# Top-k attention with expert routing on one core: the steps of the search one place further apart

## The chip, the core and the metric

The kernel runs on one core of a Trainium2 chip. The core has five engines that each take their own instructions in order and wait for one another only through semaphores: TensorE (PE in the profile, with its weight loads as PEld), VectorE (DVE), ScalarE (ACT), GpSimd (POOL) and SyncE (SP, which here only starts transfers). The metric is the device time of one execution in microseconds (us), lower is better.

## The reference

Two blocks follow one another, all in float32. The first is attention over 8 batches, 8 heads, 576 rows and head size 64, in which each row keeps only its 32 largest scores:

```python
scores = scale * np.matmul(q, k.transpose(0, 1, 3, 2))
kth = np.partition(scores, -top_k, axis=-1)[..., -top_k:-top_k + 1]
scores = np.where(scores >= kth, scores, -1000000000.0)
attn = softmax(scores)             # over the last axis
x = np.matmul(attn, v)             # heads side by side: 4608 x 512
```

The second block routes each of the 4608 rows of x to the best of 8 experts, keeps the 80 rows with the largest gate weight of each expert, and sends those through two matrix products (512 to 1024 to 512); all other rows of the output are zero.

## The kernel before

**Work and staging.** Two heads of one batch form a head pair; there are 32, numbered n. The 576 rows of a head pair are cut into four tiles of 128 rows and one of 64. A *unit* i is one head of one 128-row tile; the 64-row tile holds both heads side by side in one unit. So a head pair has 9 units (four times two, and one), and the whole attention has NU = 288. Only after it come routing and experts (from about 868 us on), which the change does not touch.

**What is done for a tile.** `front` (L226) multiplies q and k into the PSUM tile `sp`, and ScalarE copies the scores to `s` (L233). `parts` takes the 8 largest of each sixth of a row into `cand` (L241). `search` finds from `cand` the 24 largest (L252, L260). Then ScalarE makes `sign` (L257), which marks the scores above the 24th, and counts them; GpSimd multiplies `y = s * sign` (L263); VectorE takes the 8 largest of `y` into `w` (L265), and `pick` (L268) chooses the 32nd largest score among these as threshold. `below` makes the `mask`: on GpSimd (L279) for units with an even number, on ScalarE (L277) for odd ones. `turn_w` transposes the scores and adds the masks on TensorE (L315, L320) into `ab` (PSUM, one buffer) and `cc` (PSUM, two buffers), and ScalarE takes the exponential into `wT` (L322 from `cc`, L324 from `ab`). `back` multiplies with v (L335), into free columns of the same `cc`. `over` takes the reciprocal of the row sums on VectorE (L347, tile `z_all`), and `divide` copies `cc` times that into `xn` on ScalarE (L358). Only then is this buffer of `cc` free. `norm` stores `xn`, transposes it (L201, L375) and multiplies it with the gate weights (L380, L387). `turn` transposes q and k of the next head pair (L201) and ScalarE copies them out as `both` (L214). All of `sp`, the transposes of `turn` and of `norm` and the small product share one PSUM buffer.

**The order** is written out by hand. The program is recorded in *steps*; step i works on unit i in `parts` and `search`, on earlier units in the later stages, and on a later one in `front` (unit i + 4). Each letter of a string stands for one piece of work, and `back` says how many units behind i it is:

```python
back = dict(a=0, b=1, c=1, d=1, e=1, y=2, g=3, h=4, m=4, H=3, M=3)
for c in "GybGcGdGeGGzag" if i % 2 else "GGbghHmMyGcGdGeGza":
```

G is a piece of L241; a, b, c, d, e are the steps of `search` up to the sign, which ScalarE gets with e; y is the product on GpSimd, g is L265, h and H are the two picks, m and M the two masks, z the reciprocal. After the letters a step issues `turn_w` of the tile whose last unit is i - 4, `divide` of the tile whose reciprocal was just taken, `front` and `back` (of the tile of unit i - 5). Every engine executes its share of this one order without overtaking. For each head pair I call the five tiles' weight turns W0 to W4; W4 is that of the 64-row tile. `cc` has two buffers, so W2 takes the buffer of W0, W3 that of W1, and so on through the head pairs.

SBUF tiles come from pools: `s` has 5 buffers (one for the two heads of a tile), `sign` 2, `mask` 3, and the small tiles 4.

Of the kernel before, what the change touches and what calls it, by code (L numbers as in the profile page):

```python
# [9 lines left out]
F32 = mybir.dt.float32  # L10
# [17 lines left out]
def kernel(  # L28
# [21 lines left out]
    P = 128  # L50
# [98 lines left out]
    class Attention:  # L149


        def __init__(self, stack, lean):
            self.lean = lean
            pool = lambda name, bufs, **kw: stack.enter_context(tc.tile_pool(name=name, bufs=bufs, **kw))
            self.nat, self.qkp, self.rows = pool("nat", 1), pool("qkp", 2), pool("rows", 2)
            self.small, vpool = pool("small", 4), pool("vpool", 1)
            self.ps_s, self.ps_w, self.ps_c = (pool(n, k, space=PSUM) for n, k in (("ps_s", 1), ("ps_w", 1), ("ps_c", 2)))
            self.qk, self.turned, self.lg = {}, {}, {}
            self.s, self.top, self.cnt, self.y, self.mask, self.w, self.xn = ({} for _ in range(7))
            self.thr, self.z = thr_all, z_all  # L160
            self.odd = set()


            self.vb = []
            for j in range(1 if lean else 3):
                t = vpool.tile([P, NK, 2, D + 1], F32, name=f"vb{j}")
                nc.gpsimd.memset(t[:, :, :, D : D + 1], 1.0)
                nc.gpsimd.memset(t[: P - TL, NF, :, :], 0.0)
                self.vb.append(t)

            self.xT = vpool.tile([P, NK * P], F32, name="xT")
            nc.gpsimd.memset(self.xT[:, S:], 0.0)

        def load(self, n, b, hp):
            one = bass.ds(b, 1)
            tiles = []
            for name, src in (("qn", q), ("kn", k)):
                t = self.nat.tile([P, NK, 2, D], F32, name=name, tag=name)
                for h in range(2):
                    nc.sync.dma_start(  # L180
                        t[:, 0:NF, h, :],
                        src[one, 2 * hp + h, : NF * P, :].rearrange("o (c p) d -> p (o c) d", p=P))
                nc.sync.dma_start(
                    t[0:TL, NF, :, :], src[one, 2 * hp : 2 * hp + 2, NF * P :, :].rearrange("o h p d -> p (o h) d"))
                tiles.append(t)
            t = self.vb[n % len(self.vb)]
            for h in range(2):
                nc.sync.dma_start(
                    t[:, :NF, h, :D], v[one, 2 * hp + h, : NF * P, :].rearrange("o (c p) d -> p (o c) d", p=P))
            nc.sync.dma_start(  # L190
                t[P - TL :, NF, :, :D], v[one, 2 * hp : 2 * hp + 2, NF * P :, :].rearrange("o h p d -> p (o h) d"))
            self.qk[n] = tiles

        def four(self):
            return self.ps_s.tile([P, 4, 512], F32, name="sp", tag="sp")
# [20 lines left out]
        def front(self, n, t):  # L216

            qT, kT = self.turned[n]
            m = P if t < NF else TL
            i = n * UPP + 2 * t  # L220
            ps = self.four()
            for j in range(2):
                for h in range(2):
                    d = slice(D * h, D * h + D)
                    o = ps[:, 2 * h + j, :HS] if t < NF else ps[TL * h : TL * h + TL, j, :HS]
                    nc.tensor.matmul(o, lhsT=qT[d, t * P : t * P + m], rhs=kT[d, j * HS : (j + 1) * HS], start=True, stop=True)  # L226
            g = 2 if t < NF else 1
            s = self.rows.tile([P, 2 * S], F32, name="s", tag="s", bufs=2 if self.lean else 5)
            for h in range(g):
                self.s[i + h] = s[:, h * S : (h + 1) * S]  # L230
            for j in range(0, 2 * g, 2 if i == 0 else 2 * g):
                w = 2 if i == 0 else 2 * g
                nc.scalar.activation(s[:, j * HS : (j + w) * HS].rearrange("p (j c) -> p j c", c=HS), ps[:, j : j + w, :HS],  # L233
                                     Act.Copy, scale=TINY)
# [10 lines left out]
        def search(self, i):  # L245

            s, cand = self.s[i], self.top[i]
            top = self.top[i] = self.small.tile([P, G0 // 8 - 1, 8], F32, name="top", tag="top")
            w9 = self.small.tile([P, 16], F32, name="w9", tag="w9")
            for r in range(G0 // 8):  # L250
                dst = top[:, r, :] if r < G0 // 8 - 1 else w9[:, :8]
                nc.vector.max(out=dst, in_=cand)  # L252
                if r == G0 // 8 - 1:

                    sign = self.rows.tile([P, S], BF16, name="sign", tag="sign")
                    cnt = self.small.tile([P, 1], F32, name="cnt", tag="cnt")
                    nc.scalar.activation(sign, s, Act.Sign, bias=w9[:, 7:8], scale=-1.0, accum_out=cnt)  # L257
                yield
                if r < G0 // 8 - 1:
                    nc.vector.match_replace(out=cand, in_to_replace=dst, in_values=cand, imm_value=LOW)  # L260
                    yield
            y = self.rows.tile([P, S], F32, name="y", tag="y")
            nc.gpsimd.tensor_tensor(out=y, in0=s, in1=sign, op=Alu.mult)  # L263
            yield
            nc.vector.max(out=w9[:, 8:], in_=y)  # L265
            yield
            pick = self.small.tile([P, TOP_K - G0 + 1], F32, name="pick", tag="pick")
            nc.vector.scalar_tensor_tensor(out=pick, in0=past, scalar=cnt, in1=w9[:, 7:], accum_out=self.thr[:, i : i + 1],  # L268
                                           op0=Alu.is_equal, op1=Alu.mult)
            yield  # L270

        def below(self, i):

            self.top.pop(i)
            self.mask[i] = self.rows.tile([P, S], BF16, name="mask", tag="mask", bufs=3)
            if i in self.odd:
                nc.scalar.activation(self.mask[i], self.s[i], Act.Relu, bias=self.thr[:, i : i + 1], scale=-1.0)  # L277
                return
            nc.gpsimd.tensor_scalar(self.mask[i], self.s[i], self.thr[:, i : i + 1], None, op0=Alu.is_lt)  # L279
# [147 lines left out]
        def run(self, slow):  # L427

            units = []
            for n in range(NP):  # L430
                for t in range(NF):
                    units += [(n, t, 0), (n, t, 1)]
                units.append((n, NF, 2))
            self.odd = set(range(1, NU, 2))
            first, second = {}, {}
            later = []
            due = []
            drawn = []
            ready = {}

            def whole(i):
# [3 lines left out]
            def step(i, last):  # L445
                if 0 <= i < NU:
                    n, t, h = units[i]
                    if t == 2 and h == 1 and n + 2 < NP:
                        self.load(n + 2, *divmod(n + 2, HP))
                    if t in (1, 3) and h == 0 and slow and n:  # L450
                        slow.pop(0)()
                    if t == 0 and h == 0 and n + 1 < NP:
                        due.append(n + 1)
                    first[i] = self.parts(i)


                back = dict(a=0, b=1, c=1, d=1, e=1, y=2, g=3, h=4, m=4, H=3, M=3)
                for c in "GybGcGdGeGGzag" if i % 2 else "GGbghHmMyGcGdGeGza":
                    if c == "G":
                        if 0 <= i < NU:  # L460
                            next(first[i])
# [3 lines left out]
                            second[i] = self.search(i)  # L465
                            next(second[i])
                    elif c == "z":
                        for u in drawn:
                            self.over(*u)
                    elif c in "mM":  # L470
                        if 0 <= i - back[c] < NU:
                            self.below(i - back[c])
                    elif i - back[c] in second:
                        next(second[i - back[c]])
                done = list(drawn)
                drawn.clear()

                def back():
                    if whole(i - 5):
                        self.back(*units[i - 5][:2])  # L480
                        drawn.append(units[i - 5][:2])


                rest = whole(i - 4) and units[i - 4][2] == 2
                if rest:
                    back()
                if whole(i - 4):
                    self.turn_w(*units[i - 4][:2])
                for u in done:
                    self.divide(*u)  # L490

                ends = [(n, range(NK) if n < NP - 1 else range(NF) if t < NF else range(NF, NK))
                        for n, t in done if t == NF or (n == NP - 1 and t == NF - 1)]
# [20 lines left out]
                    ready[later[-1]] = 0  # L514

            with tc.manual_schedule():
                self.load(0, 0, 0)
                self.load(1, *divmod(1, HP))
                nc.sync.dma_start(wg, moe_w_gate.rearrange("(c p) e -> p c e", p=P))
                self.turn(0)  # L520
                i = -4
                while i < NU + 6 or later:
                    step(i, i >= NU + 5)
                    i += 1
            assert not slow and not due

        def batch(self, b):

            for hp in range(HP):
                self.load(hp, b, hp)  # L530
                self.turn(hp)
                for t in range(NK):
                    self.front(hp, t)
# [381 lines left out]
```

## Time and profile before

| | us |
|---|---|
| median of 3 runs (lowest, highest) | 994.47 (993.04, 995.51) |
| the profiled execution | 994.13 |
| its span, first to last instruction | 992.4 |
| busy in the span: PE, DVE, ACT, POOL | 881.3, 804.6, 798.2, 627.3 |
| first and last GpSimd mask start | 22.12, 855.23 |
| mean granted TensorE clock | 0.983 of full speed |

The profile is of one execution. Its own time lies 1.7 us above its span (launch and end), and 0.3 us below the median of the runs. Busy times of different engines overlap. The row of a group of instructions gives their count, the busy time and the mean duration of one, and then the idle time of that engine just before them with what ended it; a row of the waits gives the waiting instruction, what released it, the time in total, how often, and the longest. In the timeline, an instruction begins often some 0.1 us before the one ahead of it on the same engine has ended, so that the distance of two starts is shorter than the duration.

### The profile page before, as it was taken

How to read it: one execution, taken by the hardware profiler on the slowest of the kernel's cores; microseconds unless marked ns; L12 is line 12 of the kernel's file. 1: busy time of each engine (PE TensorE's matmuls, PEld its weight loads, DVE VectorE, ACT ScalarE, POOL GpSimd, SP SyncE). 2: the span in 40 equal slices, each digit the busy share in tenths (PEclk: the TensorE clock that was granted, in tenths of full speed). 3: DMA queues.
4: the chain of work that ended last, by engine and by line, in shares of the span. 5: the costliest groups of instructions: out<-in, count | busy, mean ns of one | idle time of the engine just before them, and what ended most of it. 6: DMA issues, size and time to landing. Idle time of an engine off the chain costs nothing.

```text
span 992.4 us, 35679 instructions
## 1 busy us (share of the span) xinstructions
PE 881.3 (89%) x13368; PEld 710.3 (72%) x13368; DVE 804.6 (81%) x4928; ACT 798.2 (80%) x1652; POOL 627.3 (63%) x474
## 2 busy tenths in 40 slices
PE   5899999999989999999899999999899998689996
PEld 3677777777767777777677777777677776578896
DVE  5798989898989898999989898989898989471110
ACT  3899999999989999999899999999899999501110
POOL 3677767676767777777677676766677777402111
PEclk9999999999999999999999999999999999979999
DMA  3445453333323233333111122222222200084921
GB/s 72 102 123 133 126 135 91 92 92 92 93 76 77 75 87 86 88 90 92 46 41 44 44 50 50 51 50 49 49 50 50 50 13 14 16 339 147 368 85 29
DMA packets 167797, 85.76 MB, mean 86 GB/s; under 512 B 117696, under 2 KB 154560, under 8 KB 167616
## 3 DMA queue, kind: packets, MB, share of 16 engines
q1 hardware_dynamic: 166592, 80.78, 29.1%
q0 software_dynamic: 1024, 2.62, 0.9%
q8 instruction: 107, 1.75, 0.7%
q14 instruction: 74, 0.61, 0.2%
HBM read 63.19 MB, written 20.19 MB: 84 GB/s over the span
## 4 chain that ended last, share of the span: by engine, by line
DVE 46%; PE 26%; ACT 15%; POOL 7%; issue 5%; DMA 1%; POOLq 0%; SPq 0%; DVEq 0%; ACTq 0%
DVE cand L241 15%; DVE w L265 11%; DVE cand L260 6%; PE cc L335 5%; DVE top L252 5%; ACT sign L257 5%; POOL y L263 5%; PE sp L226 4%; PE yp L799 4%; DVE pick L268 3%; ACT wT L324 3%; ACT mask L277 3%; PE sp L201 2%; DVE w L252 2%; POOL mask L279 2%
## 5 line engine op out<-in xcount | busy, mean ns | idle before, releaser
L241 DVE MAX8 cand<-s 128x8 f32<-128x96 f32 x1728 | 400.6, 246 | 9.0 <-ACT s L233 8.8
L263 POOL TENSOR_TENSOR y<-s,sign 128x576 f32<-128x576 f32 x288 | 365.3, 1280 | 65.9 <-ACT sign L257 65.9
L279 POOL TENSOR_SCALAR mask<-s,thr_all 128x576 bf16<-128x576 f32 x144 | 247.9, 1722 | 178.3 <-DVE pick L268 175.4
L335 PEld LDWEIGHTS cc<-vb,wT 128*64 128x64 f32 x5760 | 182.8, 139 | 113.6 <-ACT wT L324 100.1
L265 DVE MAX8 w<-y 128x8 f32<-128x576 f32 x288 | 216.4, 752 | 45.8 <-POOL y L263 45.8
L335 PE MATMUL cc<-vb,wT 128*64 128x65 f32 x5760 | 205.2, 226 | 42.7 <-ACT wT L324 42.7
L257 ACT ACTIVATE sign<-s,w 128x576 bf16<-128x576 f32 x288 | 225.2, 782 | 7.1 <-POOL y L263 3.0
L226 PE MATMUL sp<-both 64*128 64x288 f32 (+1 forms) x1280 | 203.2, 437 | 17.5 <-ACT part L387 9.5
L233 ACT ACTIVATE s<-sp 128x1152 f32<-128x1152 f32 (+1 forms) x161 | 167.4, 1040 | 12.2 <-PE sp L226 9.9
L315 PE MATMUL ab<-ident,s 128*128 128x128 f32 x1148 | 176.2, 283 | 0.0
L324 ACT ACTIVATE wT<-ab 128x1024 f32<-128x1024 f32 (+1 forms) x159 | 149.1, 937 | 0.0
L226 PEld LDWEIGHTS sp<-both 64*128 64x128 f32 (+1 forms) x1280 | 106.1, 180 | 56.4 <-ACT part L387 11.4
L315 PEld LDWEIGHTS ab<-ident,s 128*128 128x128 f32 x1148 | 127.9, 142 | 11.6 <-issue 0.9
L252 DVE MAX8 top<-cand 128x8 f32<-128x48 f32 x576 | 116.0, 201 | 4.5
L277 ACT ACTIVATE mask<-s,thr_all 128x576 bf16<-128x576 f32 x144 | 112.4, 781 | 6.9 <-DVE pick L268 6.5
L320 PEld LDWEIGHTS <-mask 128*128 128x128 bf16 x1440 | 94.2, 98 | 31.9 <-POOL mask L279 29.2
L260 DVE MATCH_REPLACE8 cand<-top,cand 128x48 f32<-128x48 f32 x576 | 110.9, 193 | 0.0
L358 ACT ACTIVATE xn<-cc,z_all 128x64 f32<-128x64 f32 (+1 forms) x320 | 86.6, 320 | 1.2 <-DVE z_all L347 0.8
L315 PE MATMUL cc<-ident,s 128*128 128x128 f32 x288 | 79.1, 275 | 0.0
L322 ACT ACTIVATE wT<-cc 128x256 f32<-128x256 f32 (+1 forms) x160 | 56.9, 356 | 16.8 <-PE cc L320 15.5
L268 DVE SCALAR_TENSOR_TENSOR pick<-past,cnt,w 128x9 f32<-128x9 f32 x288 | 60.3, 223 | 0.3 <-ACT xn L358 0.3
L257 ACT ACTIVATION_READ_ACCUMULATOR sign<-s,w 128x1 f32 x288 | 58.7, 204 | 0.0
(187 smaller groups left out, 909.4 us busy)
## 6 DMA issues: line engine op xcount, KB each, us to landing
w<-in_moe_w_dram SPq DMA_DIRECT2D x10, 2048.0 KB, 11.6
w<-in_moe_w_dram SPq DMA_DIRECT2D x24, 512.0 KB, 4.6
out_dram<-zero SPq DMA_DIRECT2D x9, 1024.0 KB, 6.5
qn<-in_q_dram SPq DMA_DIRECT2D x64, 128.0 KB, 2.5
kn<-in_k_dram SPq DMA_DIRECT2D x64, 128.0 KB, 2.5
vb<-in_v_dram SPq DMA_DIRECT2D x64, 128.0 KB, 2.7
xd<-xn SPq DMA_DIRECT2D x32, 256.0 KB, 3.8
qn<-in_q_dram SPq DMA_DIRECT2D x32, 32.0 KB, 2.3
```

The costliest lines, as they stand in the source:

```text
L226: nc.tensor.matmul(o, lhsT=qT[d, t * P : t * P + m], rhs=kT[d, j * HS : (j + 1) * HS], start=True, stop=True)
L233: nc.scalar.activation(s[:, j * HS : (j + w) * HS].rearrange("p (j c) -> p j c", c=HS), ps[:, j : j + w, :HS], Act.Copy, scale=TINY)
L241: nc.vector.max(out=cand[:, j, :], in_=s[:, j * S // NG : (j + 1) * S // NG])
L252: nc.vector.max(out=dst, in_=cand)
L257: nc.scalar.activation(sign, s, Act.Sign, bias=w9[:, 7:8], scale=-1.0, accum_out=cnt)
L260: nc.vector.match_replace(out=cand, in_to_replace=dst, in_values=cand, imm_value=LOW)
L263: nc.gpsimd.tensor_tensor(out=y, in0=s, in1=sign, op=Alu.mult)
L265: nc.vector.max(out=w9[:, 8:], in_=y)
L279: nc.gpsimd.tensor_scalar(self.mask[i], self.s[i], self.thr[:, i : i + 1], None, op0=Alu.is_lt)
L315: nc.tensor.matmul(dst[h][c], lhsT=sc[:, keys[c]], rhs=ident, start=c == 0 or (c == NF and h == 0), stop=False, is_transpose=True, skip_gr ...
L324: nc.scalar.activation(wT[:, : g * NF, :], ab.rearrange("p h c r -> p (h c) r")[:, : g * NF, :], Act.Exp, scale=scale / TINY)
L335: nc.tensor.matmul(cc[r : r + TL, o], lhsT=wT[:, h * NF + c if c < NF else 2 * NF + h, r : r + TL], rhs=vb[:, c, h if t < NF else r // TL, ...
```

## The change

It moves stages of the order to later steps, adds buffers, and splits the loading of v from that of q and k. No instruction is added or removed in the attention; their order on each engine changes. The product y moves from 2 to 3 units behind, L265 from 3 to 4; the pick and mask of odd units from 3 to 5, those of even units stay at 4 (the letters h, m and H, M change places in parity). `turn_w` moves from 4 to 6 units behind, `back` from 5 to 7, and the reciprocal comes two steps after `back` in place of one, earlier within its step; `divide` is issued ahead of `turn_w` of the same step, where it was behind it. The loading of v for head pair n + 2 is issued two steps later.

```diff
-            self.small, vpool = pool("small", 4), pool("vpool", 1)
+            self.small, vpool = pool("small", 7), pool("vpool", 1)
...
-            s = self.rows.tile([P, 2 * S], F32, name="s", tag="s", bufs=2 if self.lean else 5)
+            s = self.rows.tile([P, 2 * S], F32, name="s", tag="s", bufs=2 if self.lean else 7)
...
-                    sign = self.rows.tile([P, S], BF16, name="sign", tag="sign")
+                    sign = self.rows.tile([P, S], BF16, name="sign", tag="sign", bufs=3)
...
-            self.mask[i] = self.rows.tile([P, S], BF16, name="mask", tag="mask", bufs=3)
+            self.mask[i] = self.rows.tile([P, S], BF16, name="mask", tag="mask", bufs=4)
...
+            LT = 6
...
-            drawn = []
+            drawn = [[], [], []]
...
                     if t == 2 and h == 1 and n + 2 < NP:
                         self.load(n + 2, *divmod(n + 2, HP))
+                    if t == 3 and h == 1 and n + 2 < NP:
+                        self.load_v(n + 2, *divmod(n + 2, HP))
...
-                back = dict(a=0, b=1, c=1, d=1, e=1, y=2, g=3, h=4, m=4, H=3, M=3)
-                for c in "GybGcGdGeGGzag" if i % 2 else "GGbghHmMyGcGdGeGza":
+                back = dict(a=0, b=1, c=1, d=1, e=1, y=3, g=4, h=5, m=5, H=4, M=4)
+                for c in "GybGczGdGeGGag" if i % 2 else "GGbghHmMyGcGdzGeGa":
...
                     elif c == "z":
-                        for u in drawn:
+                        for u in drawn[0]:
                             self.over(*u)
...
-                done = list(drawn)
-                drawn.clear()
+                done = drawn.pop(0)
+                drawn.append([])
+                for u in done:
+                    self.divide(*u)
 
                 def back():
-                    if whole(i - 5):
-                        self.back(*units[i - 5][:2])
-                        drawn.append(units[i - 5][:2])
+                    if whole(i - LT - 1):
+                        self.back(*units[i - LT - 1][:2])
+                        drawn[1].append(units[i - LT - 1][:2])
 
-                rest = whole(i - 4) and units[i - 4][2] == 2
+                rest = whole(i - LT) and units[i - LT][2] == 2
                 if rest:
                     back()
-                if whole(i - 4):
-                    self.turn_w(*units[i - 4][:2])
-                for u in done:
-                    self.divide(*u)
+                if whole(i - LT):
+                    self.turn_w(*units[i - LT][:2])
...
-                while i < NU + 6 or later:
-                    step(i, i >= NU + 5)
+                while i < NU + LT + 3 or later:
+                    step(i, i >= NU + LT + 2)
```

The function `load_v` holds the three transfers of v that stood at the end of `load`, and is called right behind `load` for the first two head pairs.

More of the change, by code (lines that the diff above doesn't have):

```diff
@@ L185, in load, with load_v @@
                 tiles.append(t)
+            self.qk[n] = tiles
+        def load_v(self, n, b, hp):
+            one = bass.ds(b, 1)
             t = self.vb[n % len(self.vb)]
@@ L191, in load @@
                 t[P - TL :, NF, :, :D], v[one, 2 * hp : 2 * hp + 2, NF * P :, :].rearrange("o h p d -> p (o h) d"))
-            self.qk[n] = tiles
         def four(self):
@@ L516, in run @@
             with tc.manual_schedule():
-                self.load(0, 0, 0)
-                self.load(1, *divmod(1, HP))
+                for n in range(2):
+                    self.load(n, *divmod(n, HP))
+                    self.load_v(n, *divmod(n, HP))
                 nc.sync.dma_start(wg, moe_w_gate.rearrange("(c p) e -> p c e", p=P))
@@ L530, in batch @@
                 self.load(hp, b, hp)
+                self.load_v(hp, b, hp)
                 self.turn(hp)
```

## The prediction

> **What bounds the kernel now.** I read the page first, then the waits of the steady stretch, then the timelines of GpSimd, TensorE and ScalarE.
>
> ```profile
> PE 881.3 (89%) x13368; PEld 710.3 (72%) x13368; DVE 804.6 (81%) x4928; ACT 798.2 (80%) x1652; POOL 627.3 (63%) x474
> ```
>
> No engine is full over the span, and four are close together. The waits between 60 and 845 us say how they hold one another (us, times, longest):
>
> ```profile
> POOL mask L279 <- DVE pick L268: 166.7, 134, 3.3
> ...
> POOL y L263 <- ACT sign L257: 45.9, 58, 2.1
> DVE w L265 <- POOL y L263: 37.8, 43, 2.1
> ...
> ACT both L214 <- PE sp L201: 21.1, 29, 2.3
> DVE z_all L347 <- PE cc L335: 19.4, 15, 1.3
> ```
>
> GpSimd, the least busy engine, waits most, and its timeline shows a ring:
>
> ```profile
> 322.15 1.72 POOL L279 TENSOR_SCALAR mask<-s,thr_all 128x576 bf16<-128x576 f32 x1 [1.14 <-DVE pick L268]
> 323.83 2.52 POOL L263 TENSOR_TENSOR y<-s,sign 128x576 f32<-128x576 f32 x2
> 327.45 1.72 POOL L279 TENSOR_SCALAR mask<-s,thr_all 128x576 bf16<-128x576 f32 x1 [1.10 <-DVE pick L268]
> ```
>
> Mask, two products, then 1.10 us for L265 and the pick that frees the next mask: 5.31 us for two units. The masks go from 22.12 to 855.23 us in 143 rounds, 5.83 us each. The 0.52 between are rounds in which the second product waits for its sign (0.6 to 2.1 us), because ScalarE is late with it: behind `both`, the transposes of `norm`, or TensorE.
>
> [...]
>
> **What the change takes away.** The sign gets a whole step more before its product, so the 45.9 us and the 37.8 us behind them (the same delay, counted once: about 46) should go; the reciprocal comes later behind `back`, so most of the 19.4 us should go too. The mask's own wait stays: mask, product, product, L265, pick is still one ring. In the new order both picks stand ahead of GpSimd's mask, where one did: 0.19 us more (starts of the two picks at 327.06 and 327.25). That ring is then 5.50 us. VectorE and GpSimd alone would give 143 x (5.83 - 5.50) = 47 us less.
>
> **What it adds: a wait for `cc`.** A weight turn may write `cc` only after `divide` of the tile two turns earlier. Before, this was done a step and more ahead; the timeline's groups on `cc` have, among those that waited for it, one line:
>
> ```profile
>   ACT xn L358: 0.8, 1
> ```
>
> One wait of 0.8 us in 785 us. In the new order the lead is one step: `turn_w` of a tile comes 6 steps after its last unit, its `divide` 9, and the turn that needs its buffer 10 (before: 4, 6 and 8). For W0, which follows the one-unit W4, it is the same step: `divide` of W3 stands directly ahead of W0's exponential on ScalarE. W4 has the same with `divide` of W2. So ScalarE and TensorE form a ring: s (L233), then masks and signs, `xn`, then TensorE's turn from its first `cc` matmul, `front`, then the next s. The pieces, from the rows:
>
> ```profile
> 605.99 0.27 PE L315 MATMUL cc<-ident,s 128*128 128x128 f32 x1
> ...
> 606.92 0.22 PE L320 MATMUL cc<-huge,mask 128*128 128x128 bf16 x1
> ...
> 607.30 1.24 PE L226 MATMUL sp<-both 64*128 64x288 f32 x8
> 608.53 1.39 PE L335 MATMUL cc<-vb,wT 128*64 128x65 f32 x40
> ```
> ```profile
> 607.18 0.38 ACT L322 ACTIVATE wT<-cc 128x256 f32<-128x256 f32 x1 [0.46 <-PE cc L320]
> ...
> 624.18 0.36 ACT L322 ACTIVATE wT<-cc 128x256 f32<-128x256 f32 x1
> 624.44 1.01 ACT L324 ACTIVATE wT<-ab 128x1024 f32<-128x1024 f32 x1
> 625.35 0.52 ACT L358 ACTIVATE xn<-cc,z_all 128x64 f32<-128x64 f32 x2
> 625.74 1.14 ACT L233 ACTIVATE s<-sp 128x1152 f32<-128x1152 f32 x1
> 626.75 0.80 ACT L277 ACTIVATE mask<-s,thr_all 128x576 bf16<-128x576 f32 x1
> 627.42 0.79 ACT L257 ACTIVATE sign<-s,w 128x576 bf16<-128x576 f32 x1
> ```
>
> From start to start: s 1.01, mask 0.67, sign with its read-out 0.76, the two xn 0.39 (they end 0.51 after their start), exponentials 0.26 + 0.90. On TensorE: first `cc` matmul to `front` 1.31, to the exponential 1.19; `front` 1.24; handing over 0.05 to TensorE and 0.04 back. So from the end of xn to the next s pass 0.05 + 1.31 + 1.24 + 0.04 = 2.64 us, in which ScalarE has only what stands between (sign 0.76, exponentials 1.16).
>
> **The sum.** I add from one s to the next, over the five turns of a head pair, in the order of the changed kernel on ScalarE and TensorE. For even n, mask and sign stand ahead of xn:
> - W0 to W1: 1.01 + 0.67 + 0.76 + 0.62 (xn of 64 rows runs at 0.31 each) + 2.64 = 5.70.
> - W1 to W2: TensorE alone, with `back` 1.32 (after it waits for nothing), ten transposes 1.58, turn 1.80, `front` 1.24 = 5.93.
> - W2 to W3: xn ends at 2.95; 0.05 + 1.31 + 1.19 (the half `front`, as at 577.37) + 0.04 give 5.54.
> - W3 to W4: half s 0.54, mask, sign, xn to 2.48; 0.05 + 0.48 (short turn) + 1.24 + 0.04 = 4.29.
> - W4 to W0: s, sign, logits copy (ends its slot at 2.08, after TensorE's small product), mask, sign, xn to 4.02; + 2.64 = 6.66.
>
> Together 28.12. For odd n, where one mask stands after xn and fills the gap: 5.03, 6.57 (ScalarE: 2.96 until the transposes are there, `both` 1.02, mask, sign, exponentials), 5.51, 3.73, 6.44, together 27.28. Two head pairs take 55.40 us.
>
> Before, the s of unit 11 starts at 37.70 and that of unit 287 at 838.22: 800.5 us for 276 units, 52.2 us per two head pairs. After: fifteen times 55.40 (831.0), a rest of three intervals (17.2), less 1.6 because the first head pair has no predecessor: 846.6, which is 46.1 more. The filling should end 1.5 us earlier (the waits of 0.8 and 2.8 us for the first products vanish, but the s copies stay spaced by `front`, which takes 2.29 us there). After the last s, no `front` stands in the ring, and the last mask comes one product and one L265 later (about 3 us), while VectorE has a lead of two steps: I count these as equal, bounds -3 and +3. So 992.4 + 46.1 - 1.5 = 1037.0 of span, and with the 1.7 us outside it 1038.7; against the median, which lies 0.3 above that execution, **1039 us**.
>
> The 47 us of the GpSimd ring do not come off this sum: its 5.50 for two units (49.5 per 18) lies below 55.40, so VectorE and GpSimd run ahead until they stand waiting for TensorE (at the reciprocal) or for signs. What is late next is named with that: `cc`.
>
> Unknown is the pace inside the ring. ScalarE's rows have a second one, where s takes 1.16 to the next start (609.01 to 610.17) and xn 0.31: 0.25 more in each of 153 intervals, +38 us, against 0 at the pace above. I take 0, to which most rows are nearest, and keep +38 as an end. Downwards, 0.8 us per head pair that other overlap saves would be 25 us less.
>
> Costed at nothing: loading v later (nine transfers of a head pair become six and three on SP; each lands in 2.3 to 2.7 us, and `back` of that head pair is two head pairs away; if a v transfer waits for its buffer, the loads and stores queued behind it on SP wait too, but the next transpose that needs them is 4 units off); the store and products of `norm`, which follow `divide` to its later step; the constants of the routing (L645 to L650, 0.6 us of GpSimd at 3.7 us), which now come behind the attention, where GpSimd idles until 893 us; the fourth mask buffer and third sign buffer, since each writer now follows its reader by at least a step.
>
> **The rivals.**
> 1. *The ring of `cc` has slack that I deny it, and the GpSimd ring decides.* For it: those waits are in the profile, and the `cc` wait is only inferred. Against: the order on ScalarE puts xn ahead of the exponential. Price: 994 - 47 = 947. Chance 0.07.
> 2. *Only the two places where xn directly precedes the exponential cost.* ScalarE idles 1.24 us at W0 and 0.41 at W4, 1.65 x 32 = 53, less 47: 1000. It decides where sign and mask fill the rest. Chance 0.05.
> 3. *The ring runs at the slow pace:* 1039 + 38 = 1077. Chance 0.08.
>
> The forecast keeps 0.80, mainly within 1018 to 1060. To hold 8 in 10 the range reaches half way towards the third and a little towards the second: 1012 to 1072. About 0.3% (3 us) is what can be told from no change here: faster 0.07, within it 0.02 (of the second rival), slower 0.91.
>
> **What would show it.** Right: among the waits, TensorE's first `cc` matmul of a turn waiting for ScalarE's xn some 90 times (six turns in ten); ScalarE waiting for `cc` about 1.2 us once per head pair, and for `sp` at L233; the sign wait on GpSimd nearly gone; VectorE waiting at the reciprocal; ScalarE and VectorE busy shares near 77%; s of units 9 apart 27 to 28 us apart. Wrong: masks on GpSimd 5.5 us apart throughout, or no xn among TensorE's releasers.

## The result and the profile after

The changed kernel takes 1075.68 us (median of 4 runs, 1075.14 to 1076.77) against 994.48 us before (4 runs): 1.0819 times as long, 95% interval 1.0800 to 1.0838. The forecast was 1039 us with a range of 1012 to 1072. The direction and the mechanism hold; the time lies 3.7 us above the range, and 37 above the forecast.

The page's busy line, of a span of 1074.2 us:

```profile
PE 908.2 (85%) x13368; PEld 719.2 (67%) x13368; DVE 822.0 (77%) x4928; ACT 804.1 (75%) x1652; POOL 626.3 (58%) x474
```

VectorE and ScalarE are busy for 77 and 75%, as foretold. TensorE has the same matmuls as before and needs 27 us more busy time for them, which was not. The waits between 60 and 925 us (us, times, longest):

```profile
POOL mask L282 <- PE cc L323: 105.9, 38, 5.3
PEld cc L318 <- ACT xn L361: 103.5, 92, 2.8
...
PE cc L318 <- ACT xn L361: 80.2, 78, 2.5
ACT wT L325 <- PE cc L323: 71.9, 77, 2.3
...
ACT s L236 <- PE sp L229: 31.4, 42, 1.2
```

(L318 and L323 are L315 and L320 of before, L361 is `xn`, L325 the first exponential, L282 GpSimd's mask.) TensorE's first `cc` matmul waits 78 times for `xn` (its weight load 92 times), ScalarE then waits for `cc` and for `sp`. That is the ring of the forecast. GpSimd no longer waits mostly for the pick (66.5 us in 38 waits); its mask waits longer for TensorE's products with the masks, whose end gives a mask tile back:

```profile
320.92 1.72 POOL L282 TENSOR_SCALAR mask<-s,thr_all 128x576 bf16<-128x576 f32 x1 [2.44 <-PE cc L323]
322.61 2.52 POOL L266 TENSOR_TENSOR y<-s,sign 128x576 f32<-128x576 f32 x2
327.92 1.72 POOL L282 TENSOR_SCALAR mask<-s,thr_all 128x576 bf16<-128x576 f32 x1 [2.80 <-PE cc L323]
```

Its two products follow one another without a gap as before; the rest of its round of 7.00 us is time in which it is held back from outside. What TensorE does in a long wait for `xn`, from its timeline at the first turn of a head pair:

```profile
634.45 0.66 PE L318 MATMUL ab<-ident,s 128*128 128x128 f32 x4
636.64 0.33 PE L318 MATMUL cc<-ident,s 128*128 128x128 f32 x1 [1.54 <-ACT xn L361]
...
638.59 2.28 PE L229 MATMUL sp<-both 64*128 64x288 f32 x8
```

The wait is 1.54 us. Behind it, `front` takes 2.28 us, where it takes 1.24 in the next turn (from 644.74 us). Three stretches of 3.4 us around it, in the order window, its length, busy time and instructions of PE, PEld, DVE, ACT and POOL, then the granted TensorE clock, the DMA share and GB/s:

```profile
633.90:637.32 3.42, 1.88 (x30) 1.62 (x29) 3.36 (x18) 2.59 (x8) 2.63 (x3) 1.00 0.39 89
637.32:640.73 3.41, 3.41 (x20) 2.22 (x18) 2.59 (x19) 1.39 (x2) 1.97 (x2) 0.50 0.29 82
640.73:644.15 3.42, 2.82 (x54) 2.43 (x53) 1.82 (x10) 3.19 (x7) 2.20 (x2) 1.00 0.00 0
```

For exactly one stretch the clock is halved. The trace's records of the granted clock have 13 such stretches between 60 and 840 us; before, there are two.

**Where the 37 us are.** The s of unit 11 starts at 35.95 us (forecast 36.2) and that of unit 287 at 915.5 (forecast 882.8): 32.7 us are lost by then. From there to the end pass 158.8 us, 4.6 more than before (forecast 0, bounds -3 and +3). Two causes offer themselves for the 32.7: the halved clock, and the pieces of the ring.

### The profile page after: what moved, and what is told of

Its sections match the earlier page's. It is cut to its first block, busy times and chain, and to the rows that moved or that the text cites. A ratio compares the mean times of both kernels' runs of the same rounds, so it can differ in the third digit from the quotient of the medians.

```text
span 1074.2 us, 35978 instructions
## 1 busy us (share of the span) xinstructions
PE 908.2 (85%) x13368; PEld 719.2 (67%) x13368; DVE 822.0 (77%) x4928; ACT 804.1 (75%) x1652; POOL 626.3 (58%) x474
## 3 DMA queue, kind: packets, MB, share of 16 engines
q8 instruction: 107, 1.75, 0.7%
## 4 chain that ended last, share of the span: by engine, by line
PE 32%; ACT 26%; DVE 21%; issue 15%; POOL 5%; DMA 1%; SPq 0%; POOLq 0%; DVEq 0%; ACTq 0%
ACT sign L260 9%; PE sp L229 7%; ACT mask L280 6%; DVE cand L244 6%; PE cc L338 6%; DVE w L268 6%; ACT wT L327 4%; POOL y L266 4%; PE yp L807 3%; PE sp L204 3%; PE ab L318 3%; ACT xn L361 3%; DVE cand L263 3%; PE ab L323 2%; DVE pick L271 2%
## 5 line engine op out<-in xcount | busy, mean ns | idle before, releaser
L282 POOL TENSOR_SCALAR mask<-s,thr_all 128x576 bf16<-128x576 f32 x144 | 247.9, 1721 | 294.2 <-PE cc L323 107.3
L338 PEld LDWEIGHTS cc<-vb,wT 128*64 128x64 f32 x5760 | 182.1, 138 | 107.2 <-ACT wT L327 88.0
L338 PE MATMUL cc<-vb,wT 128*64 128x65 f32 x5760 | 204.4, 225 | 34.7 <-ACT wT L327 33.0
L260 ACT ACTIVATE sign<-s,w 128x576 bf16<-128x576 f32 x288 | 221.9, 771 | 0.4
L229 PE MATMUL sp<-both 64*128 64x288 f32 (+1 forms) x1280 | 214.6, 457 | 6.4 <-ACT s L236 4.5
L318 PE MATMUL ab<-ident,s 128*128 128x128 f32 x1148 | 181.2, 283 | 0.0
L318 PE MATMUL cc<-ident,s 128*128 128x128 f32 x288 | 85.3, 296 | 83.1 <-ACT xn L361 81.6
L229 PEld LDWEIGHTS sp<-both 64*128 64x128 f32 (+1 forms) x1280 | 112.3, 190 | 50.0 <-ACT s L236 7.9
L318 PEld LDWEIGHTS ab<-ident,s 128*128 128x128 f32 x1148 | 128.2, 142 | 10.2 <-issue 0.8
L325 ACT ACTIVATE wT<-cc 128x256 f32<-128x256 f32 (+1 forms) x160 | 57.1, 357 | 79.1 <-PE cc L323 78.7
L318 PEld LDWEIGHTS cc<-ident,s 128*128 128x128 f32 x288 | 40.8, 142 | 105.4 <-ACT xn L361 105.4
L323 PEld LDWEIGHTS <-mask 128*128 128x128 bf16 x1440 | 100.8, 103 | 2.3
L361 ACT ACTIVATE xn<-cc,z_all 128x64 f32<-128x64 f32 (+1 forms) x320 | 85.1, 311 | 1.2 <-DVE z_all L350 0.8
L350 DVE RECIPROCAL z_all<-cc 128x2 f32<-128x2 f32 (+1 forms) x160 | 25.9, 162 | 52.4 <-PE cc L338 50.2
```

What stands on the lines that cost most here:

```text
L318: nc.tensor.matmul(dst[h][c], lhsT=sc[:, keys[c]], rhs=ident, start=c == 0 or (c == NF and h == 0), stop=False, is_transpose=True, skip_gr ...
L338: nc.tensor.matmul(cc[r : r + TL, o], lhsT=wT[:, h * NF + c if c < NF else 2 * NF + h, r : r + TL], rhs=vb[:, c, h if t < NF else r // TL, ...
```

## The experiments

My theory: the ring of `cc` makes the kernel slow, at the pieces that the forecast added up, and on top of it the waits of that ring drop TensorE's clock. The rivals: the deeper search, the second pick, the buffers or the later loads are the cause. All times are medians.

| kernel | us | ratio to before (95%) |
|---|---|---|
| before + buffers + v later | 991.93 | 0.9986 (0.9973 to 1.0000) |
| before + reciprocal and `divide` later | 1053.15 | 1.0597 (1.0572 to 1.0623) |
| changed, `divide` one step earlier | 1022.13 | 1.0286 (1.0261 to 1.0310) |
| changed, `divide` placed as before | 996.12 | 1.0025 (1.0014 to 1.0036) |
| changed + 8 warm-up matmuls | 1054.54 | 1.0616 (1.0591 to 1.0641) |
| changed + 3 warm-up matmuls | 1072.76 | 1.0785 (1.0760 to 1.0810) |

**The buffers and v alone.**

```diff
+ s bufs 5 -> 7, sign 2 -> 3, mask 3 -> 4, small 4 -> 7
+ load_v(n + 2) two units behind load(n + 2)
```

> The kernel before with nothing changed but the added SBUF buffers (s 7, sign 3, mask 4, small tiles 7) and v loaded two units later. Theory (the ring of `cc` and the clock that drops in its waits make the changed kernel slow): these parts are worth nothing, 994 us, within 4. Rival (the buffers or the later loads cost or bring something): outside 990 to 998; were they the cause of the loss, above 1030.

991.93 us: no difference that this measurement can tell, as the theory said. GpSimd's wait for the sign is 44.6 us in 57 waits (45.9 in 58 before). So a third sign buffer removes almost none of it. The gap that repeats, the mask's wait for the pick, stays too: 154.4 us in 123 waits (166.7 in 134 before). A lack of SBUF buffers is not the reason of this gap here.

**Only `divide` later, in the kernel before.**

```diff
-            drawn = []
+            drawn = [[], []]
...
-                        for u in drawn:
+                        for u in drawn[0]:
...
-                done = list(drawn)
-                drawn.clear()
+                done = drawn.pop(0)
+                drawn.append([])
...
-                        drawn.append(units[i - 5][:2])
+                        drawn[1].append(units[i - 5][:2])
...
+                for u in done:
+                    self.divide(*u)
                 if whole(i - 4):
                     self.turn_w(*units[i - 4][:2])
-                for u in done:
-                    self.divide(*u)
```

> The kernel before with only reciprocal and `divide` one step later behind `back`, and `divide` ahead of `turn_w` as in the changed kernel; the search is not deepened, and the buffers stay. Theory (ring of `cc`): the ring is there with all its pieces, so 1040 to 1085 us, with xn among the releasers of TensorE's first `cc` matmul. Rival (the deeper search, the second pick ahead of GpSimd's mask, or the mask tiles that TensorE releases): 994 us, within 10.

1053.15 us, with the shallow search, the old buffers and v as it was. Its waits between 60 and 880 us:

```profile
POOL y L263 <- ACT sign L257: 108.9, 131, 1.7
...
PEld cc L315 <- ACT xn L358: 98.5, 102, 1.5
```

The ring is there 102 times, and GpSimd's waits for signs have grown from 45.9 to 108.9 us: ScalarE, held by the ring, is late with them. The ring alone, without the deeper search, makes a slow kernel. These 59 us hold two things at once, `divide` one step later and its place ahead of the exponentials; the next two runs take them apart.

**The changed kernel with `divide` one step earlier, in two placings.** The first edit:

```diff
-                        drawn[1].append(units[i - LT - 1][:2])
+                        drawn[0].append(units[i - LT - 1][:2])
```

> The changed kernel with only reciprocal and `divide` moved one step earlier, so that they follow `back` by one step as in the kernel before; all else stays as changed (deeper search, turn of weights six steps behind, buffers, v later). Theory (ring of `cc`): the lead over `cc` is two steps again, xn vanishes among TensorE's releasers, and the ring of GpSimd with both picks ahead of its mask decides at 5.50 us for two units: 947 by that, up to 975 with what remains of the waits for `sp`. Rival (deeper search, second pick, mask release): 1075, within 15.

1022.13 us: 53.5 less than the changed kernel, so this one step is two thirds of the loss; but 28 above before, outside what either theory said. Between 60 and 880 us TensorE waits as follows:

```profile
PEld cc L338 <- ACT wT L327: 143.7, 125, 3.5
...
PEld cc L318 <- ACT xn L361: 10.9, 15, 0.7
```

The wait for `xn` falls from 92 times to 15. In its place TensorE waits at `back` for the exponentials (143.7 us, 80.8 in the changed kernel), which stand behind `xn` on ScalarE. So the second edit puts these back too (z at the end of the letters, `divide` behind `turn_w`):

```diff
-"GybGczGdGeGGag" if i % 2 else "GGbghHmMyGcGdzGeGa"
+"GybGcGdGeGGzag" if i % 2 else "GGbghHmMyGcGdGeGza"
...
-                for u in done:
-                    self.divide(*u)
...
                 if whole(i - LT):
                     self.turn_w(*units[i - LT][:2])
+                for u in done:
+                    self.divide(*u)
```

> The changed kernel with reciprocal and `divide` in the places of the kernel before: one step behind `back`, the reciprocal at the end of a step's VectorE work, `divide` behind `turn_w`. Deeper search, six steps to the turn, buffers and v as changed. Left of the change is then only the search, one step deeper. Theory A (the 28 us that the kernel with the earlier `divide` is slower than before come from xn standing ahead of the exponentials on ScalarE, so that `back` starts later): 994 or less, down to 960. Theory B (they come from the deeper search itself, whose order of signs, picks and masks lengthens ScalarE's way from s to s): 1010 to 1030.

996.12 us. The remaining 26 us were the places of `xn` and the reciprocal, as theory A said for their origin. The edit moves the two together, so their shares stay open. But A's range, 960 to 994, is missed at its slow end, and B's 1010 was too much: the deeper search is worth nothing. It does what it was to do. Between 60 and 845 us no wait of GpSimd's product for a sign is left in the list; the longest waits of `back` and of the mask are:

```profile
PEld cc L338 <- ACT wT L327: 106.6, 120, 1.5
POOL mask L282 <- DVE pick L271: 65.6, 46, 3.3
```

GpSimd waited 166.7 us for picks before and waits 65.6 now, and its masks still come 5.84 us apart (5.83 before). The time did not go: in 60 to 820 us GpSimd is busy for 548.8 us, where it was 551.9, so it stands idle as long as before; its mask now waits for TensorE (L338 34.8 us, L323 31.4), VectorE's `cand` (34.6) and others. Its waits were slack.

**How slack they were.** In the kernel before, one swap of letters puts the even unit's pick ahead of L265 of the odd unit:

```diff
-"GGbghHmMyGcGdGeGza"
+"GGhbgHmMyGcGdGeGza"
```

> The kernel before with one swap in VectorE's order: the pick of the even unit stands ahead of L265 of the odd one, so that GpSimd's mask no longer waits for the product that runs just before it. If the ring of GpSimd (mask, two products, L265, pick: 5.31 of 5.83 us for two units) decides the time: up to 1.10 us less in each of 143 rounds, 840 to 960 us. If ScalarE's own work decides (47 to 50 us of 52 for eighteen units by its timeline): 985 to 994, the waits of GpSimd only change their name.

1001.77 us (ratio 1.0071, 1.0054 to 1.0089). Its waits (60 to 845 us):

```profile
POOL y L263 <- ACT sign L257: 93.0, 112, 1.8
POOL mask L279 <- DVE pick L268: 82.5, 95, 3.2
```

The pick's wait has halved, the sign's has doubled, and the kernel is 7 us slower, outside both ranges. The "ring of GpSimd", with which the forecast opened, does not set the time. Swapping the two picks and masks in the kernel of 996.12 us shows the same:

```diff
-"GGbghHmMyGcGdGeGza"
+"GGbgHhMmyGcGdGeGza"
```

> As the kernel with reciprocal and `divide` as before, with the even unit's pick and mask ahead of the odd unit's: GpSimd's mask comes 0.19 us earlier. If GpSimd's ring decides there: 10 to 27 us faster than that kernel. If it does not: within 4 us of it.

997.06 us, the same within 1 us.

What sets the time before? Over 60 to 820 us (window, length, then busy time of PE, PEld, DVE, ACT, POOL) the kernel before has:

```profile
60.00:820.00 760.00, 690.96 (x10010) 548.01 (x10009) 698.37 (x4380) 710.71 (x1468) 551.90 (x392) 1.00 0.28 73
```

ScalarE is busy for 93.5% of it, VectorE for 91.9, TensorE for 90.9. The shares over the whole span (80, 81, 89%) hide this, because they include 125 us of routing and experts in which ScalarE and VectorE do little. To see whether ScalarE decides, two masks in nine changed sides.

```diff
-self.odd = set(range(1, NU, 2))
+self.odd = {i for i in range(1, NU, 2) if i % 18 not in (5, 15)}    # two to GpSimd
+self.odd = {i for i in range(NU) if i % 2 or i % 18 in (4, 14)}    # two to ScalarE
```

> The kernel before with the added buffers and v later, and two of the nine masks of eighteen units that ScalarE makes (those of the 6th and 16th unit) made by GpSimd instead: 32 masks of 0.67 us off ScalarE, 1.72 us each on GpSimd. If ScalarE's own work decides (busy 93.5% of the steady stretch): up to 21 us faster than the 992 of that kernel, 970 to 985. If the ring of GpSimd decides: 32 times 1.72, up to 55 us slower.

> The opposite: two of the nine masks of eighteen units that GpSimd makes (those of the 5th and 15th) made by ScalarE. If ScalarE decides: 32 times 0.67, 21 us slower than 992, 1005 to 1015. If the ring of GpSimd decides: up to 55 us faster.

1014.16 us (1.0216, 1.0188 to 1.0244) and 1007.81 us (1.0139, 1.0111 to 1.0167): both slower than the 991.93 of the same kernel with its masks as they were. Two masks more cost ScalarE 16 of the 21 us worked out, which speaks for ScalarE. Two fewer cost 22, which is the other branch of that forecast; there TensorE's turns wait longer for GpSimd's masks (its weight load for a mask 55.2 us in 75 waits, 29.0 in 36 with the masks as they were). ScalarE deciding, with GpSimd so close behind it that it takes over at once, is one reading; neither run shows it. VectorE, busy for 91.9%, is a rival that no run tested, and the chain of work that ended last speaks for it. The page of before gives that chain by engine:

```profile
DVE 46%; PE 26%; ACT 15%; POOL 7%; issue 5%; DMA 1%; POOLq 0%; SPq 0%; DVEq 0%; ACTq 0%
```

So which engine sets the time of the kernel before stays open; that it is not the ring of GpSimd is what the runs show. With the deeper search it is no better, with the same two masks or with four (`not in (3, 5, 13, 15)`):

> The kernel with the deeper search and reciprocal and `divide` as before (996 us), with the same two masks of ScalarE given to GpSimd. If the deeper search loosens GpSimd, as its ring was meant to be, and ScalarE decides: 965 to 980, faster than the same edit on the kernel before. If the deeper search is worth nothing with that either: as much less as there, within 4 us.

> As the last one, with four masks of nine given to GpSimd (4th, 6th, 14th and 16th unit): another 21 us off ScalarE. If ScalarE still decides: 950 to 970. If TensorE (busy 91%) or VectorE (92%) decide by then: no faster than with two masks, within 5 us.

1015.34 and 1059.21 us. The first costs 19 us against 996.12, where the same edit cost 22 without the deeper search: the second branch, so the deeper search does not loosen GpSimd. The second lies far outside what I had allowed. The waits point to GpSimd there too: VectorE's L265 waits for its product 0.2 us in all in the kernel of 996.12 us, 45.7 with two masks moved and 82.0 with four (60 to 845 us). That this wait makes the loss is not shown.

**The turn of weights five steps behind.**

```diff
-            LT = 6
+            LT = 5
```

> As the kernel with reciprocal and `divide` as before, and the turn of weights five steps behind the unit rather than six, that is in the step of the masks, as in the kernel before. If the extra step of the turn costs nothing: the same within 5 us. If masks come too late for a turn in their own step: 10 to 40 us slower.

1063.08 us against 996.12: 67 slower, more than I had allowed for late masks. TensorE's `front` waits 53.6 us (28 times) for ScalarE's `xT`, which it does not in the kernel of 996.12 us. With five steps the turns fall into steps of the other parity, in which other work stands beside them; that this is the cause is argued, not shown.

**The clock.** Eight matmuls on zeros in the first turn of each head pair, ahead of its first `cc` matmul:

```diff
-    WARM1, WARM2 = 92, 22
+    WARM0, WARM1, WARM2 = 8, 92, 22
...
                 for c in range(NK):
+                    if t == 0 and h == 0 and c == NF and n and not self.lean:
+                        z16 = zero.bitcast(BF16)
+                        for _ in range(WARM0):
+                            nc.tensor.matmul(ab[:, 1, 0:2, :].rearrange("p c r -> p (c r)"), lhsT=z16[:, :P], rhs=z16,
+                                             start=True, stop=True)
```

> The changed kernel with eight small bf16 matmuls on zeros (256 columns each, some 0.9 us together, into the part of `ab` that the same turn overwrites next) in the wait of the first turn of each head pair, just ahead of its first `cc` matmul; nothing else changes. Theory (the granted clock drops behind waits of 1.3 to 1.6 us there, and each drop costs 1.6 us): the waits shrink to some 0.5 us, the drops vanish, 1050 us, between 1044 and 1060. Rival (the drops are not caused by the wait, or the loss is in the handing over alone): 1073 to 1085, and the intervals of 8.3 us behind the fifth turn stay.

1054.54 us, 21.1 less, by adding work. Its TensorE timeline:

```profile
620.64 1.04 PE L321 MATMUL ab<-zero 128*128 128x256 bf16 x8
622.35 0.33 PE L323 MATMUL cc<-ident,s 128*128 128x128 f32 x1 [0.67 <-ACT xn L366]
...
623.71 1.24 PE L229 MATMUL sp<-both 64*128 64x288 f32 x8
```

A wait of 0.67 us remains, `front` takes 1.24 us, and the granted clock from 60 to 820 us is 1.00, where it is 0.97 in the changed kernel. The intervals from s to s that were 8.0 to 8.3 us are 6.7 and 6.5 now, and the medians of all others are the same to 0.01 us. That settles the clock's share.

With three matmuls:

```diff
-    WARM0, WARM1, WARM2 = 8, 92, 22
+    WARM0, WARM1, WARM2 = 3, 92, 22
```

> As the run with eight warm-up matmuls, with three of them: the waits of 1.5 and 1.3 us at the first turn of a head pair shrink to about 1.2 and 1.0. If the clock drops behind waits over 1.3 us alone: 1054 us, within 3, as with eight. If any idle time counts in proportion: half of the gain, 1060 to 1068.

1072.76 us. Both expectations fail: the waits there are 1.22 and 1.00 us long, where they were 1.54 and 1.33, and the mean granted clock of the span is 0.970, against 0.968 in the changed kernel and 0.988 with eight matmuls. Here it is not the single wait over 1.3 us that counts (see the last section).

**`front` ahead of the turn.** To see by which way the ring closes, `front` was recorded ahead of `turn_w`, in the changed kernel, in the kernel before with buffers and v, and in that of 996.12 us.

```diff
+                if busy:
+                    self.front(*units[f][:2])
                 if whole(i - LT):
                     self.turn_w(*units[i - LT][:2])
-                if busy:
-                    self.front(*units[f][:2])
```

> The changed kernel with `front` (its matmuls and its copy s) ahead of the turn of weights in each step, nothing else. Theory (the ring goes from xn over the turn from its first `cc` matmul, 1.31 us, and `front`, 1.24 us, to the next s): s no longer waits for the turn, `front` fills TensorE's wait for xn, and the clock stays up; what is left is ScalarE's own work: 985 to 1015. Rival (the ring is closed by another way, over the exponentials and `back` to the reciprocal and xn): 1050 or more, since the copy s then stands ahead of the exponentials and makes that way 1.01 us longer.

> The same order (`front` ahead of the turn) in the kernel before with the added buffers and v later, as a control without the ring of `cc`. If the order by itself is worth nothing: 992, within 5. If s ahead of the exponentials delays `back`: 1000 to 1030.

> The same order in the kernel with the deeper search and reciprocal and `divide` as before (996 us). There TensorE makes ScalarE wait for `cc` and `sp`, 37 us in the steady stretch; with `front` earlier the 18 us for `sp` go: 975 to 990, faster than both kernels. If the exponentials, now behind s, delay `back` by as much: 996 to 1010.

1170.55, 1132.74 and 1177.32 us: the order itself costs 141 and 181 us where the ring is absent, far more than either branch allowed, so the first run (95 us more than the changed kernel) can't be read as it was meant. In the control, between 60 and 845 us:

```profile
PE cc L338 <- ACT wT L327: 121.8, 103, 1.5
```

TensorE now stands idle at `back` for the exponentials 103 times, up to 1.5 us (32.4 us in 57 waits with `front` in its old place): by the order, `front` was what filled that time. One thing can be taken from the pair of the changed kernel and its version without the ring: in this order the changed places of reciprocal and `divide` cost nothing (1170.55 against 1177.32), and in the changed kernel with this order TensorE's weight load for `cc` waits for `xn` 2.5 us in 10 waits, where it was 103.5 in 92. Where `front` does not lie on the way from `xn` to s, the ring does not bind. That agrees with the forecast's way, but these kernels have another bound, so it does not show it.

## Why the prediction was right and where it failed

**Right.** What the change adds was named and priced as the cause: the lead of `divide` over `cc`, waits of TensorE for `xn` some 90 times (92), ScalarE's waits for `cc` and `sp`, busy shares near 77%, most sign waits gone (45.9 to 13.1 us), the filling 1.5 us earlier (1.75). That GpSimd's gains could not come off the sum held too. With the clock held up, the intervals can be set beside the forecast's own; these are medians of the run with eight warm-up matmuls:

| interval | even n: forecast, measured | odd n: forecast, measured |
|---|---|---|
| W0 to W1 | 5.70, 5.77 | 5.03, 5.17 |
| W1 to W2 | 5.93, 5.93 | 6.57, 6.79 |
| W2 to W3 | 5.54, 5.61 | 5.51, 5.51 |
| W3 to W4 | 4.29, 4.41 | 3.73, 3.75 |
| W4 to W0 | 6.66, 6.72 | 6.44, 6.51 |
| sum | 28.12, 28.44 | 27.28, 27.73 |

**Failed, by size:**
1. *A term that is missing, 21 us: the clock.* The sum took TensorE's rows (1.31 for the turn, 1.24 for `front`) at full clock, and the same sum leaves TensorE waiting for `xn` at the first turn of a head pair (1.54 and 1.33 us in the trace). That these waits would lower the clock I did not count, though the page of before has it at 0.983 and not 1. This is the step of the forecast that failed most: TensorE's rows behind those waits do not run at the pace of the rows before (`front` 2.28 us against 1.24). Measured: 13 halved stretches, (879.5 - 858.9) / 13 = 1.6 us each, where 879.5 and 858.9 are the times from the s of unit 11 to that of unit 287 without and with the eight matmuls.
2. *The pieces of the ring, 12 us.* 56.17 instead of 55.40 per two head pairs, 0.77 times 15.3. No interval is off by more than 0.22 us. One piece shows in the rows of the warm run above: from the first `cc` matmul behind its wait to `front` pass 1.36 us (622.35 to 623.71), where the sum has 1.31; the rest I have not traced. The forecast put the unknown pace at +38 or 0 and took 0; the intervals lost 12. Its third rival, a slow pace throughout, lands at the measured time (1077), but by luck: the table excludes 38, and the clock and the end make up the difference.
3. *The end, 4.6 us* instead of 3 at most: ScalarE's last copy of logits ends 31.8 us after the start of the last s, where it was 27.9 before; 1.9 of the 4.6 went with the warm-up matmuls.

**Also wrong, without effect on the sum:** "VectorE and GpSimd alone would give 47 us less", and with it the first rival's 947. The kernel of 996.12 us is the nearest to that rival's case: the ring of `cc` is all but absent (10.9 us in 15 waits for `xn`), the product's waits for signs are gone, and nothing is gained. I read GpSimd's repeating wait as the ring that bounds the kernel, when it was slack: in the steady stretch ScalarE, VectorE and TensorE are busy for 91 to 93.5%, GpSimd for 73%. I had taken busy shares over the whole span, where no engine looked full. Two smaller statements fail too. Most of the 19.4 us of VectorE's waits at the reciprocal were to go; they are 39.9 us in 27 waits. And GpSimd, running ahead, was to stand at signs; it stands at its mask tiles (105.9 us), though the forecast costed the added buffers at nothing because each writer follows its reader by a step.

**The whole in three steps:** before 994; the search one step deeper, the buffers and v, 996; `xn` ahead of the exponentials and the reciprocal earlier in its step, 1022 (+26); one step more from `back` to `divide`, 1076 (+54, of which 21 are the clock). No kernel tried beats the one before by more than can be measured.

## What to carry to other kernels

Before giving a stage more lead, look whether its result lives in a buffer that another stage must write: two PSUM buffers held one step longer cost 54 us here (21 of them through the clock), and the added SBUF buffers did not prevent it. Busy shares are to be taken over the steady stretch. An engine with a regular wait need not be the bound: GpSimd's wait for the pick was halved twice here, and neither kernel was faster. Where a forecast makes TensorE wait once per head pair for 1.3 to 1.5 us, as here, the clock of the stretch behind it belongs into the sum (13 halved stretches here, 1.6 us each).

## What the runs showed of the hardware

During the attention of the changed kernel the granted clock goes to 0.50 for one stretch of 3.41 us at a time, 13 times between 60 and 840 us; behind the attention it stays there for up to three such stretches in a row (10.24 us from 947.93). Of the 12 distances between the starts of the 13, nine are 58.0 us and three 85.3, 17 and 25 times the length of a stretch. The 13 intervals from s to s that hold a halved stretch take 7.97 to 8.34 us; the same intervals of other head pairs, without one, take 6.7 us for even n and 6.5 for odd. With the time laid out in stretches of this length from those starts, the one just ahead of each drop in the changed kernel has 1.33 to 2.55 us in which TensorE stands idle; in the kernel before it is 2.10 and 2.00 us ahead of its two. Idle time alone does not decide: five stretches of the changed kernel with 1.54 us idle had no drop behind them, and three with 1.33 to 1.46 us had one. What else counts is open, and so is why the interval of 6.7 us became 8.0 to 8.3 us in 9 of 15 even head pairs and not in the other six.
